# Attention and two feed-forward layers in one kernel: the values' products are issued one item later, transposed probabilities get a fourth room, and the masks read the thresholds where they are kept

## The chip, the core and the metric

The kernel runs on one core of one Trainium2 chip. The metric is device time in microseconds (us): the median of three runs of the kernel before is 1247.12 us (lowest 1243.89, highest 1250.25). One execution was profiled; it took 1249.53 us, of which the trace covers a span of 1247.8 us. Every time in this document that is read from the trace is on the clock of that span. PE is the matmul engine and PEld its weight load, DVE, ACT and POOL are the three engines that work on vectors, and SP issues the transfers (DMA). SPq in a row is SP's queue.

## The reference

Attention over 4 batches, 8 heads, 576 positions and head size 64, with a bias that a small network computes from the two positions; then two feed-forward layers over the 2304 tokens:

```python
scores = q @ k.T / sqrt(64)                              # (4, 8, 576, 576)
x = log1p(|i - j|) / log1p(max(i, 1))                    # (576, 576)
bias = relu(x[..., None] @ w1 + b1) @ w2                 # 32 hidden units, 8 heads
attn = softmax(scores + bias)                            # over j
y = (attn @ v) as (2304, 512)
y = (silu(y @ w_gate) * (y @ w_val)) @ w_out             # 512 -> 1536 -> 512
out = relu(y @ w_in) ** 2 @ w_out2                       # 512 -> 2048 -> 512
```

## The kernel before

**Numbers in two halves.** Almost every operand is held as two float16 numbers, a high part and the rest, and a product takes three matmuls (high by high, high by rest, rest by high). This is why one item of the attention needs a pair of probability halves, `pt`, and a transposed pair of them, `pT`.

**The attention's passes and items.** The 576 queries are worked on in five passes: t = 0, 1, 2 and 3 of 128 queries each, and a pass "m" in which the last 64 queries of two heads lie together. An item is one head of one batch (in pass m a pair of heads), so passes 0 to 3 have 32 items each and pass m has 16. This document numbers the 112 items from pass 1 on: 0 to 31 in pass 1, 32 to 63 in pass 2, 64 to 95 in pass 3 and 96 to 111 in pass m. Pass 0 is written differently: it takes its probabilities in float32, transposes them on PE and normalises by sums that it has beforehand.

**One item, step by step.** `scores` (L801): 4 matmuls (8 in pass m) into one of two PSUM rooms `qk`. `soft` (L820): DVE adds the bias and finds the extreme (L824), ACT takes the exponential into one of three rooms `s` (L832), then ACT or POOL, in turn, makes the high half in one of three rooms `pts` (L839, L836). `soft2` (L842): POOL makes the rest of it with two subtractions (L859 and L860, both recorded under the helper's line L220), then SP issues a transposing DMA from `pt` to `pT` (L861), one of three rooms. `weighted` (L864): 14 matmuls (28 in pass m) of `pT` with the values (L877). `normalise` (L882) divides on DVE, once per four items.

**The order in which an item's steps are written.** `attend` (L934) holds items back in two lists. In the turn of item k it writes the scores of k; then, if the list `pend_av` holds two items, the values' products of the oldest; then `soft` of k; then `soft2` of k-1, which puts k-1 on that list. So the products of item k-3 are written behind the scores of item k (L986). At the end of a pass the list is emptied: the products of all items that are left are written before the next pass begins (L1010).

**Between them.** `attend` is a generator, and `merge` (L1018) lets it take turns with `make_bias` for the next pass (the masks, L605, their products, L644, and the evacuation, L609), by costs written beside the `yield`s. The first feed-forward layer (`moe1`, L427: its matmuls are at L459 and L482) runs beside it as soon as 256 tokens (a "unit") are through the attention. The loop at L1321 picks which of the two streams is continued. The framework then takes this written order as priorities and sets the order of each engine's instructions itself, by its own model of their times; each engine then works its list strictly in order. A matmul that waits for its operand therefore holds up all matmuls behind it on PE, and a DMA issue that waits holds up all issues behind it on SP.

**Rooms.** Tiles of a pool that share a tag take turns in `bufs` rooms, and one that finds no free room waits for the last reader. The pool `att` lives through the attention. The pool `pre` (L1050) holds things of pass 0 and is closed at its end; the pool `strm` (L1128) is then opened in its place, for the keys, values and outputs of passes 1 to m. The second layer's weights (`weights2`, L1229) are loaded and decoded after the attention's pools are closed, and the second layer (`hidden`, `outputs`) runs from about 890 us to the end.

**The masks.** `bias_setup` computes one threshold per hidden unit and query into `thetas` (L546). `make_bias` (L586) sets one column of the spare tail of the pass's bias room to zero (L592), copies the pass's 128 thresholds there (L594) and compares a table with that copy, once per 32 keys of a query block (L605).

Of the kernel before, what the change touches and what calls it, by code (L numbers as in the profile page):

```python
# [11 lines left out]
F16 = mybir.dt.float16  # L12
# [9 lines left out]
B, H, S, D = 4, 8, 576, 64  # L22
DM, FF1, FF2 = 512, 1536, 2048
NT = B * S
P = 128
# [50 lines left out]
def tile_attention_moe(  # L76
# [4 lines left out]
    nc = tc.nc  # L81
# [20 lines left out]
    st = {}  # L102
# [291 lines left out]
    att = a_stack.enter_context(tc.tile_pool(name="att", bufs=2, side="right"))  # L394
# [108 lines left out]
        nc.sync.dma_start(y_d[m][P * t:P * t + P, :], yh.rearrange("p l e -> p (l e)"))  # L503


    BW = 8 * S + P
    rooms = [gv.tile([P, BW], F32, name="room0"), att.tile([P, BW], F32, name="room1", bufs=1)]
    w2a = rooms[0][:, 0:9 * 512].rearrange("p (a b) -> p a b", b=512)
    scrap = att.tile([P, 2112 + (TAB + TAB2) // 2], F32, name="scrap", bufs=1)
# [76 lines left out]
    def make_bias(t):  # L586

        merged = t == "m"
        i0, ni = (512, 64) if merged else (P * t, P)
        nh = 4 if merged else 8  # L590
        bias = rooms[{0: 1, 1: 0, 2: 1, 3: 0, "m": 1}[t]]
        nc.gpsimd.memset(bias[:, 8 * S:8 * S + 1], 0.0)  # L592
        theta = bias[:, 8 * S:8 * S + P // 2].bitcast(F16)[:, 0:ni]
        nc.vector.tensor_copy(theta, thetas[:, i0:i0 + ni])  # L594
        bias = bias[:, 0:nh * S].rearrange("p (h j) -> p h j", h=nh)
        st["bias", t] = bias
        xs = scrap[:, 1536:1536 + S]
# [242 lines left out]
        return s, pt  # L840

    def soft2(s, pt, warm=None):  # L842
        pT = att.tile([P, 10, P], F16, tag="pT", name="pT", bufs=3)
        if pt is None:
            pf = pT.rearrange("p a i -> p (a i)").bitcast(F32)
            tr = ps_qk.tile([P, 2, 512], F32, tag="qk", name="tr")
            if warm is not None and av_done[0] < 14:

                for _ in range(2):
                    nc.tensor.matmul(  # L850
                        tr[:, 0, :], ident_h, warm[:, 0:4, :], start=True, stop=True)
            for c in range(4):
                nc.tensor.transpose(tr[:, 0, P * c:P * c + P], s[:, P * c:P * c + P], ident)

            nc.tensor.transpose(tr[:, 1, 0:P], s[:, S - P:S], ident)
            nc.scalar.copy(pf, tr.rearrange("p a j -> p (a j)")[:, 0:640])
            return pf.rearrange("p (c i) -> p c i", i=P)

        rest_of(pt[:, 1, 64:S], s[:, 0:512], pt[:, 0, 0:512])  # L859
        rest_of(pt[:, 1, 0:64], s[:, 512:S], pt[:, 0, 512:S])  # L860
        nc.sync.dma_start_transpose(out=pT[:, 0:9, :], in_=pt.rearrange("p l j -> p (l j)"))  # L861
        return pT

    def weighted(t, pT, av, slot, vs):  # L864
# [69 lines left out]
    def attend(u0, t, bs, big, feed):  # L934
# [43 lines left out]
        for idx, (b, n) in enumerate(items):  # L978
# [4 lines left out]
            else:  # L983
                kts = [hold["k", b, n // 2][:, n % 2, :]]
            pq = scores(t, b, n, kts)
            if len(pend_av) == 2:  # L986
                yield from avstep(*pend_av.pop(0))
            yield 0.5
            total = None
# [499 lines left out]
```

## Time and profile before

| | |
|---|---|
| median of three runs | 1247.12 us |
| lowest, highest | 1243.89, 1250.25 us |
| the profiled execution, and its span | 1249.53 us, 1247.8 us |
| mean granted TensorE clock | 0.955 of full speed |
| PE busy | 1098.1 us, 88% of the span |
| PEld, DVE, ACT, POOL busy | 65%, 62%, 55%, 53% |
| the page's chain of waits, by engine | PE 44%, DMA 15%, POOL 9%, DVE 8%, ACT 5% |
| of it the transposes of the probabilities, and of the queries | 5%, 3% |

The shares are means over stages that differ: passes 1 to m run from 284 to 759 us, the second layer's weights are prepared around 770 to 890 us, and from 945 us on PE is busy nearly all the time. So each stage is read for itself. In a row that begins with an engine, a bracket at its end tells how long that engine sat idle before it and what ended the idle time.

### The profile page before, as it was taken

The numbers are of one execution on the slowest core, as the hardware profiler recorded it, in microseconds if no ns is written. First come the engines' busy times: TensorE is split into PE (matmuls) and PEld (weight loads), VectorE is DVE, ScalarE is ACT, GpSimd is POOL, SyncE is SP. The second block draws the span as 40 slices with busy tenths as digits, with TensorE's granted clock in tenths as the row PEclk, the third lists the DMA queues.
The fourth block names the chain that finished last, engine by engine and source line by source line (L and its number), as shares of the span: only waits on it lengthen the run. The fifth ranks groups of instructions, "written<-read, shape, count | busy, mean of one in ns | idle before, by whom it ended". The sixth has DMA issues, their size and how long they took to land.

```text
span 1247.8 us, 27388 instructions
## 1 busy us (share of the span) xinstructions
PE 1098.1 (88%) x10550; PEld 813.0 (65%) x10550; DVE 778.5 (62%) x1872; ACT 681.4 (55%) x1386; POOL 656.6 (53%) x842
## 2 busy tenths in 40 slices
PE   2587889999668889999997899979889999999998
PEld 2466778687457578686774767556348476584787
DVE  6998857787677566666575745886473442624423
ACT  4467877647667556656564543366452643616433
POOL 2532213269877688878685462136782541705423
PEclk9678889999989999999999999989999999999999
DMA  8867644219999999997979994660001010010100
GB/s 233 196 166 196 206 113 105 51 50 189 225 203 215 215 202 185 217 198 165 184 158 251 243 235 126 202 204 1 17 20 32 18 43 26 15 38 18 26 27 18
DMA packets 278079, 163.22 MB, mean 131 GB/s; under 512 B 233276, under 2 KB 246588, under 8 KB 277948
## 3 DMA queue, kind: packets, MB, share of 16 engines
q1 hardware_dynamic: 277948, 161.46, 56.1%
q8 instruction: 83, 1.36, 0.5%
q14 instruction: 48, 0.39, 0.1%
HBM read 92.13 MB, written 19.48 MB: 89 GB/s over the span
## 4 chain that ended last, share of the span: by engine, by line
PE 44%; DMA 15%; POOL 9%; DVE 8%; ACT 5%; issue 5%; SPq 1%; POOLq 0%; ACTq 0%; DVEq 0%
PE mm L1377 12%; PE mm L459 11%; PE mm L1409 10%; DMA pT<-pt 5%; DMA qT<-qs 3%; POOL pt L220 2%; PE mm L482 2%; POOL x L1189 2%; PE ma L1409 2%; PE av L877 2%; PE qk L815 1%; DMA w2s<-in_moe_w_out_dram 1%; DMA wr<-in_v_dram 1%; DMA w2s<-in_moe_w_in_dram 1%; DMA scrap<-in_moe_w_in_dram 1%
## 5 line engine op out<-in xcount | busy, mean ns | idle before, releaser
L459 PE MATMUL mm<-xT,wr 128*128 128x256 f16 x2400 | 292.5, 278 | 13.2 <-DVE th L470 6.8
L459 PEld LDWEIGHTS <-wr 128*128 128x128 f16 x2592 | 254.0, 100 | 54.7 <-issue 18.4
L1189 POOL TENSOR_TENSOR x<-x 128x256 f32<-128x256 f32 (+1 forms) x160 | 143.0, 905 | 177.9 <-ACT x L1386 171.5
L220 POOL TENSOR_TENSOR pt<-s,pt 128x512 f16<-128x512 f32 x224 | 172.8, 795 | 35.6 <-ACT pt L839 31.5
L220 POOL TENSOR_TENSOR z<-th,z 128x256 f16<-128x256 f32 x108 | 81.4, 755 | 122.9 <-ACT z L444 117.5
L482 PE MATMUL mm<-wr,z 128*128 128x512 f16 x612 | 142.1, 379 | 0.6 <-DVE th L470 0.6
L824 DVE CUSTOM_DVE_ANT_0 s<-qk,room 128x576 f32<-128x576 f32 x144 | 107.7, 749 | 38.7 <-PE qk L815 24.0
L1409 PEld LDWEIGHTS <-wr 128*128 128x128 f16 x1134 | 110.7, 98 | 20.5 <-DVE wr L1189 3.0
L832 ACT ACTIVATE s<-s,sc 128x576 f32<-128x576 f32 x112 | 85.9, 772 | 59.3 <-DVE sc L831 45.1
L1189 DVE TENSOR_TENSOR wr<-x,wr 128x768 f16<-128x768 f32 (+3 forms) x60 | 75.4, 1268 | 64.5 <-ACT wr L1196 63.4
L1377 PE MATMUL mm<-wr,w2r 128*128 128x512 f16 (+1 forms) x480 | 103.2, 366 | 6.5 <-ACT x L1382 6.5
L482 PEld LDWEIGHTS <-z 128*128 128x128 f16 x648 | 60.0, 98 | 65.4 <-issue 1.7
L1377 PE MATMUL mm<-wr,room 128*128 128x512 f16 (+1 forms) x480 | 100.1, 358 | 0.0
L877 PE MATMUL av<-vp,pT 128*128 128x65 f16 (+3 forms) x1792 | 69.3, 195 | 34.5 <-DMA pT<-pt 31.1
L605 DVE TENSOR_TENSOR scrap<-scrap,room 128x1024 f16<-128x1024 f16 (+1 forms) x108 | 85.3, 804 | 22.5 <-PE ma L644 16.5
L877 PEld LDWEIGHTS <-pT 128*128 128x128 f16 (+1 forms) x1792 | 60.1, 101 | 51.0 <-DMA pT<-pt 41.1
L621 POOL TENSOR_TENSOR scrap<-scrap 128x256 f32<-128x256 f32 (+1 forms) x90 | 64.4, 715 | 49.7 <-ACT scrap L620 45.6
L1377 PEld LDWEIGHTS <-w2r 128*128 128x128 f16 x480 | 47.7, 99 | 54.3 <-issue 10.4
L644 PEld LDWEIGHTS <-scrap 128*128 128x128 f16 x1440 | 60.3, 105 | 25.6 <-DVE scrap L605 13.9
L1377 PEld LDWEIGHTS <-room 128*128 128x128 f16 x480 | 47.1, 98 | 45.9 <-issue 0.7
L444 ACT CAST z<-th 128x256 f16<-128x256 f32 x108 | 42.9, 399 | 62.4 <-DVE th L470 62.0
L1428 ACT ACTIVATE ob<-ob,fac 128x256 f32<-128x256 f32 x36 | 17.8, 506 | 105.5 <-DVE ob L1427 105.5
(289 smaller groups left out, 2169.6 us busy)
## 6 DMA issues: line engine op xcount, KB each, us to landing
kp<-kT_d SPq DMA_DIRECT2D x64, 288.0 KB, 3.4
vp<-v_d SPq DMA_DIRECT2D x48, 325.0 KB, 3.5
w2s<-in_moe_w_out_dram SPq DMA_DIRECT2D x16, 512.0 KB, 3.9
wr<-in_moe_w_gate_dram SPq DMA_DIRECT2D x24, 256.0 KB, 4.5
wst<-in_moe_w_out_dram SPq DMA_DIRECT2D x12, 512.0 KB, 4.5
wr<-in_moe_w_val_dram SPq DMA_DIRECT2D x24, 256.0 KB, 4.1
v_d<-vp SPq DMA_DIRECT2D x16, 325.0 KB, 2.9
y_d<-yh SPq DMA_DIRECT2D x18, 256.0 KB, 2.6
```

Source lines behind the costliest of these rows:

```text
L220: nc.gpsimd.tensor_tensor(out=out_, in0=x, in1=hi, op=ALU.subtract)
L459: nc.tensor.matmul(pg[:, 256 * gi:256 * gi + 256], wr.parts(key, f // 4, cc, wl, P * (f % 4), P), mov(xl, cc), start=k == 0, stop=k == 11)
L482: nc.tensor.matmul(po, zall[:, f, zl, P * t:P * t + P], wr.parts("o", 0, f, wl), start=k == 0, stop=k == 3 * NF1 - 1)
L605: nc.vector.tensor_tensor(out=m[:, :, ni * e:ni * e + ni], in0=block(kb, i0, ni), in1=th, op=ALU.is_gt)
L621: nc.gpsimd.tensor_tensor(out=tmp[r], in0=tmp[r], in1=xb, op=ALU.mult)
L644: nc.tensor.matmul(pv[:, :, :, c:c + 4], m[:, a, :], bd[:, l], start=l == 0, stop=l == 1)
L824: nc.vector.tensor_tensor_reduce(out=s.rearrange("p (a j) -> p a j", a=2), in0=pq[:, :, 0:288], in1=bias[:, n].rearrange("p (a j) -> p a j ...
L832: nc.scalar.activation(s, s, AF.Exp, bias=nm, scale=-1.0)
L877: nc.tensor.matmul(av[r, slot, 0:cn], pT[:, 5 * l + c, r], vs[e][c][:, c0:c0 + cn], start=m == 0, stop=m == 13)
L1189: (nc.gpsimd if how else nc.vector).tensor_tensor(out=out_, in0=a, in1=b, op=op)
L1377: nc.tensor.matmul(ph[:, :n], w2r.parts("w", g // 4, cc, wl, P * (g % 4), P), yt[:, 4 * yl + cc, :], start=m == 0, stop=m == 11)
L1409: nc.tensor.matmul(po, HS[f][:, o:o + P], st["C7"][f][wl][:, b:b + 256], start=f == 0 and k == 0, stop=f == 7 and k == 2)
```

## The change

It has three parts. From pass 1 on, the list `pend_av` is let grow to three items before the oldest one's products are written, so that they stand behind the scores of the fourth item after theirs instead of the third. `pT` of these passes moves from the pool `att` (three rooms of ten 128-column blocks) to `strm`, with four rooms of nine blocks; pass 0 keeps three rooms, now in `pre`. And the masks compare with `thetas` itself: the copy, its zeroed column and the 128 spare columns of both bias rooms go.

```diff
-    BW = 8 * S + P
+    BW = 8 * S
...
-        nc.gpsimd.memset(bias[:, 8 * S:8 * S + 1], 0.0)
-        theta = bias[:, 8 * S:8 * S + P // 2].bitcast(F16)[:, 0:ni]
-        nc.vector.tensor_copy(theta, thetas[:, i0:i0 + ni])
+        theta = thetas[:, i0:i0 + ni]
...
     def soft2(s, pt, warm=None):
-        pT = att.tile([P, 10, P], F16, tag="pT", name="pT", bufs=3)
         if pt is None:
+            pT = pre.tile([P, 10, P], F16, tag="pT", name="pT", bufs=3)
...
-        nc.sync.dma_start_transpose(out=pT[:, 0:9, :], in_=pt.rearrange("p l j -> p (l j)"))
+        pT = st["strm"].tile([P, 9, P], F16, tag="pT", name="pT", bufs=4)
+        nc.sync.dma_start_transpose(out=pT, in_=pt.rearrange("p l j -> p (l j)"))
...
-            if len(pend_av) == 2:
+            if len(pend_av) == (2 if t == 0 else 3):
```

The number of matmuls is the same; DVE and POOL have five instructions less each. What moves is the order. In the changed program a line stands one or two lines higher (L815 is L813, L877 is L876, L605 is L603, L644 is L642).

On PE in pass 3, before: the products of item 73 (`pT_8957`), first-layer matmuls (`z`), the scores of item 77 (`qk_9097`), the products of item 74 (`pT_8993`).

```order
L877 LDWEIGHTS pT_8957
L877 MATMUL av_8972<-vp_8716,pT_8957 128x65
L877 MATMUL av_8972<-vp_8716,pT_8957 128x64
L482 LDWEIGHTS z_124
L482 MATMUL mm_9072<-wr_97,z_124 128x512
L815 LDWEIGHTS qT_8842
L815 MATMUL qk_9097<-kp_8997,qT_8842 128x288
L877 LDWEIGHTS pT_8993
L877 MATMUL av_8972<-vp_8875,pT_8993 128x65
L877 MATMUL av_8972<-vp_8875,pT_8993 128x64
```

The same place in the changed program; the scores of item 77 stand ahead of these rows, and `qk_9157` holds those of item 78. `pT_8928` is item 73, `pT_8976` item 74.

```order
L876 LDWEIGHTS pT_8928
L876 MATMUL av_9040<-vp_8722,pT_8928 128x65
L876 MATMUL av_9040<-vp_8722,pT_8928 128x64
L642 LDWEIGHTS scrap_116
L642 MATMUL ma_9100<-bd_118,scrap_116 128x16x4
L482 LDWEIGHTS z_124
L482 MATMUL mm_9028<-wr_97,z_124 128x512
L813 LDWEIGHTS qT_8818
L813 MATMUL qk_9157<-kp_9147,qT_8818 128x288
L876 LDWEIGHTS pT_8976
L876 MATMUL av_9040<-vp_8860,pT_8976 128x65
L876 MATMUL av_9040<-vp_8860,pT_8976 128x64
```

The products of item 74 moved behind the scores of item 78: 174 matmuls stand between its scores and its products, and 122 did before.

On PE where pass 1 ends and pass 2 begins, before: the products of item 26 (`pT_5349`), the first two scores of pass 2 (`qk_5751`, `qk_5823`), the products of item 27 (`pT_5437`).

```order
L877 LDWEIGHTS pT_5349
L877 MATMUL av_5297<-vp_5190,pT_5349 128x65
L877 MATMUL av_5297<-vp_5190,pT_5349 128x64
L815 LDWEIGHTS qT_5741
L815 MATMUL qk_5751<-kp_5743,qT_5741 128x288
L459 LDWEIGHTS wr_97
L459 MATMUL mm_5861<-xT_4615,wr_97 128x256
L815 MATMUL qk_5823<-kp_5743,qT_5741 128x288
L877 LDWEIGHTS pT_5437
L877 MATMUL av_5297<-vp_5190,pT_5437 128x65
L877 MATMUL av_5297<-vp_5190,pT_5437 128x64
```

The same two scores in the changed program (`qk_5745`, `qk_5815`); `pT_5606` is item 31, the last of pass 1.

```order
L876 LDWEIGHTS pT_5606
L876 MATMUL av_5608<-vp_5492,pT_5606 128x65
L876 MATMUL av_5608<-vp_5492,pT_5606 128x64
L482 LDWEIGHTS z_124
L482 MATMUL mm_6114<-wr_97,z_124 128x512
L813 LDWEIGHTS qT_5735
L813 MATMUL qk_5745<-kp_5737,qT_5735 128x288
L813 MATMUL qk_5815<-kp_5737,qT_5735 128x288
```

The first scores of pass 2 stood between the products of items 26 and 27 and now stand behind those of item 31: pass 1 is emptied first. From them to item 32's products there were 181 matmuls, and now there are 62.

On DVE at the start of the program, as a piece of the difference (`thetas` are the thresholds, `room_115` and `room_114` the two bias rooms).

```order
 L562 SCALAR_TENSOR_TENSOR sc<-sc,keep_197 128x16
 L566 COPY bd<-sc 32x16 x4
-L594 COPY room_115<-thetas 128x128
-L594 COPY room_114<-thetas 128x128
+L603 TENSOR_TENSOR scrap<-scrap,thetas 128x1024 x2
 L567 COPY bd<-sc 32x16 x4
-L605 TENSOR_TENSOR scrap<-scrap,room_115 128x1024 x3
```

The first two masks moved ahead of four small copies, and two copies are gone.

## Rows read from the trace of the kernel before

**Rows 1.** Windows: us; busy us of PE, PEld, DVE, ACT, POOL; clock; DMA; GB/s

```profile
284.00:334.00 50.00, 42.68 (x527) 30.05 (x525) 36.42 (x89) 33.30 (x75) 48.69 (x66) 1.00 1.00 206
334.00:380.00 46.00, 31.30 (x419) 25.62 (x419) 33.15 (x94) 28.72 (x65) 31.29 (x45) 0.85 1.01 214
380.00:472.00 92.00, 79.72 (x945) 61.41 (x943) 57.67 (x172) 55.33 (x115) 69.65 (x93) 0.98 1.02 210
472.00:664.00 192.00, 180.45 (x2172) 140.59 (x2171) 122.75 (x372) 118.27 (x263) 153.49 (x236) 0.99 0.95 188
664.00:710.00 46.00, 37.12 (x419) 26.94 (x415) 30.57 (x93) 21.63 (x41) 18.89 (x25) 0.96 1.06 254
```

**Rows 2.** The tile pT: count, ns min/median/max, first and last start; then waiters

```profile
L861 SPq DMA_TRANSPOSE pT<-pt x112: 1242/1363/3493, 284.2 to 754.0; - x112
L867 PE MATMUL av<-room,pT x120: 219/275/422, 124.7 to 217.8; 128*128 128x64 f32 x120
...
  PE av L877: 31.1, 32
...
DMA to landing us min/median/max: 3.2/4.0/7.5
```

**Rows 3.** Waits of PE, 284 to 334 us: total us, times, longest

```profile
PE av L877 <- DMA pT<-pt: 5.7, 7, 1.1
```

**Rows 4.** Waits of PE, 334 to 380 us

```profile
PE av L877 <- DMA pT<-pt: 7.6, 4, 3.9
```

**Rows 5.** Waits of PE, 380 to 472 us

```profile
PE av L877 <- DMA pT<-pt: 6.1, 9, 1.9
```

**Rows 6.** Waits of PE, 472 to 664 us

```profile
PE av L877 <- DMA pT<-pt: 5.3, 7, 1.4
```

**Rows 7.** Waits of PE, 664 to 710 us

```profile
PE av L877 <- DMA pT<-pt: 6.4, 5, 2.4
```

**Rows 8.** Waits of SP's queue, 284 to 760 us

```profile
SPq L861 <- POOL scrap L621: 27.8, 17, 2.9
...
SPq L770 <- PE av L877: 12.9, 12, 2.4
```

**Rows 9.** Timeline, start of the program: start us, us, instruction, count [idle before]

```profile
16.42 0.30 DVE L594 COPY room<-thetas 128x128 f16<-128x128 f16 x2
...
18.16 1.04 PE L644 MATMUL qk<-bd,scrap 128*128 128x64 f16 x16 [5.63 <-DVE scrap L605]
```

**Rows 10.** Timeline, pass 3: scores, transpose and products of item 75

```profile
575.14 0.63 PE L644 MATMUL ma<-bd,scrap 128*128 128x64 f16 x16
...
578.20 0.65 PE L815 MATMUL qk<-kp,qT 128*128 128x288 f16 x4
...
587.96 1.32 SPq L861 DMA_TRANSPOSE pT<-pt  x1
...
592.16 0.60 PE L877 MATMUL av<-vp,pT 128*128 128x65 f16 x14 [1.42 <-DMA pT<-pt]
```

**Rows 11.** Timeline, pass 1 to 2: scores and products of item 32

```profile
399.18 0.65 PE L815 MATMUL qk<-kp,qT 128*128 128x288 f16 x4 [0.15 <-DMA kp<-kT_d]
...
401.12 2.78 PE L459 MATMUL mm<-xT,wr 128*128 128x256 f16 x24
...
413.49 4.91 PE L482 MATMUL mm<-wr,z 128*128 128x512 f16 x22
...
418.24 0.31 PE L877 MATMUL av<-vp,pT 128*128 128x65 f16 x5
```

**Rows 12.** Timeline, pass 3 to m: scores and products of item 96

```profile
667.22 0.68 PE L810 MATMUL qk<-kp,qT 128*64 128x288 f16 x8
...
686.37 0.63 PE L877 MATMUL av<-vp,pT 128*64 128x65 f16 x28 [1.66 <-DMA pT<-pt]
```

**Rows 13.** The chain that ended last: start us, us, what

```profile
773.14 4.43 DMA w2s<-in_moe_w_in_dram
...
1046.82 41.44 PE mm L1377 x192
```

## The prediction

> **What bounds the kernel now.** I read the windows by stage first, since the shares of the whole span mix unlike stages. The change touches passes 1 to m. There PE is the busiest engine, but not evenly [rows 1]: it is busy for 180.45 of 192 us in the long middle stretch (472 to 664 us), 79.72 of 92 before that, and only 31.30 of 46 between 334 and 380 us, where its clock also fell to 0.85. At the head of pass 1 another engine is full: POOL with 48.69 of 50 us.
>
> Next I asked what PE waits for. The list of the tile `pT` puts 31.1 us of idle PE in front of the values' products, with the transposed probabilities as the releaser [rows 2]. A transpose lands 4.0 us after its issue at the median, 7.5 at worst. Split by stretch the 31.1 us are 5.7, 7.6, 6.1, 5.3 and 6.4 [rows 3 to 7], and none after 710 us. This is all that later products can take out; PE has the same matmuls before and after.
>
> Then the items. In the middle stretch, item 75's scores end at 578.85 us and its products start at 592.16, of which PE idled 1.42 [rows 10]: the item's own way (softmax, rest, transpose) took 13.3 us and the matmuls between filled 11.9 of them. So the length of two ways is what matters: L, from an item's scores to the landing of its `pT`, which other engines set, and W, the PE work that the order puts between scores and products. PE idles where L is longer than W.
>
> Last, the chain of waits: behind the attention come loads of the second layer's weights, then PE without a gap [rows 13]. What PE gains or loses before 760 us therefore reaches the end nearly one for one.
>
> **The change part by part.** *The masks.* Five copies and five settings of a column go. Only the first two copies stand on a path: they cost DVE 0.30 us just before the first masks, for which PE was idle 5.63 us [rows 9]. Term: -0.3 us, bounds -0.3 and 0. The masks themselves keep shape, type and count, and both operands stay in the same memory; I price that at nothing.
>
> *The move of `pT`.* Same transposes, same size; pass 0 keeps three rooms. The new rooms lie where pass 0's things lay, so the first could have to wait for pass 0's products; those had ended soon after 217.8 us and the first transpose is issued at 284.2 [rows 2]. Zero, with 66 us to spare.
>
> *The fourth room.* SP's waits say whether the third room was short. Those of the transposes (L861) end with POOL's work, while waits for PE's products stand only at the loads of the values, L770 [rows 8]. No transpose waited for a room by this list; the room alone is worth nothing, and it only permits the new order. Those value loads move with the products: the room that they wait for comes free one item later, and what needs them is issued one item later too. Queued behind them on SP are transposes, so a load that waits longer would hold these up; the 12.9 us of such waits were spread over 12 loads, and I put the difference at zero.
>
> Here I weighed a rule of the Trainium skill, Perfetto Trace Analysis, section Optimization Strategy: a gap that repeats on the engine that should be full can mean that there is not enough memory for the next tile, such as too few buffers. By it most of the 31.1 us would go, and the sum would be about -31 in place of mine. The trace disagrees: the repeated gap ends with a landing, and not with a room.
>
> *The order on PE.* This is the change. I counted the matmuls that the built order puts between each item's last score and its first product, and priced them by rows: 0.11 us for a first-layer matmul of 256 columns and 0.22 of 512, 0.13 for a score (4 in 0.65 us, with the last one's tail), 0.04 for a product or a mask product [rows 10, 11]. W then comes out, before and after, as:
>
> - items 0 to 13 (to 334 us): 16.0 and 16.0. The order is the same instruction for instruction: here the framework's own times put the products, not the list's length. The 5.7 us stay.
> - items 14 to 23 (334 to 380): 11.3 and 11.7. Three waits make up the 7.6 us, the longest 3.9. Term -1, bounds -3 and +1.5 (one item, 19, has 1.5 us less in front of it).
> - items 24 to 45 (380 to 472): 14.5 falls to about 12.8. Pass 1 is now emptied before pass 2 begins. Item 32 shows the most: 19.0 us from the start of its scores to its products [rows 11], filled with 17.7 us of work, of which 11.9 are left. But this L was long because, by the order, the products of five older items were still outstanding when its scores were issued; with three, item 75 needed 13.3, and now item 32 has none ahead of it. If L shrinks as W does, nothing is lost; if not, each of about six rounds of this stretch (92 us by some 15) loses 1.7, that is 10 us. I take +2, near the first end, because the row with fewer items ahead has the shorter L.
> - items 46 to 61 and 66 to 91 (most of 472 to 664): 12.6 and 13.8 rise to 16.6 and 17.4. Item 75's 1.42 us of waiting vanish under 3.5 us more of work, and so do the others: the longest wait is 1.4 and the added work is three to four. Of the 5.3 us I leave 0.7 to items 62 to 65, where pass 2 is emptied, and take most of the rest. Term -4, bounds -4.6 and -2.
> - items 62 to 65: 13.3 falls to 11.2. Term +0.7, bounds 0 and +2.
> - items 92 to 98 (664 to 710): 11.4 and 12.4, but item 96 has 2 us less in front of it, and it waited 1.66 us with an L of 18.5 [rows 12]. Term -0.5, bounds -3 and +3.
> - items 99 to 111: 14.5 and 17.4; no wait to remove.
>
> Sum: -0.3 - 1 + 2 - 4 + 0.7 - 0.5 = -3.1 us. Against the profiled execution that is 1249.5 - 3.1 = 1246.4. That execution was 2.4 us above the median of the runs, 1247.1; from the median the sum gives 1244.0, which is my forecast. Less than 0.5%, 6.2 us, can't be told from no change by runs that spread from 1243.9 to 1250.3.
>
> Why so little of 31 us? The order gets its slack where PE hardly waits (5.3 us in 192), and gets next to none where it waits most (334 to 380, 664 to 710), since there the framework placed the products when it thought them ready, whatever the list.
>
> **The rivals.** *Faster, 1235.* The slack also reaches the stretches where PE waits most: a PE that is later in one round gives the front of the next rounds time, and the waits of 334 to 472 and 664 to 710 halve. That is half of 7.6 + 6.1 + 6.4, 10 us, with 4 in the middle: 14 less two lost at the emptied passes makes -12. The clock of 0.85 between 334 and 380 us speaks for some more, if the wait of 3.9 us is what lowered it. Against it stands the order, which puts only 0.4 us of new work there, and POOL, full just before. The least that this kind could give is all waits kept and -4; the most is all 25.4 us behind 334, or 1222.
>
> *A room was short, 1216.* If transposes started late for want of a room, the fourth ends every wait for them: all 31.1 us, 1247.1 - 31.1 = 1216. Against it stands that no wait of L861 ends with PE [rows 8], and that the order of items 0 to 13 is unchanged, so that their 5.7 us can only go by an earlier issue. This is what the page's rule would make of the gaps.
>
> *Slower, 1256.* The mechanism is the emptied passes. Items 24 to 45 lose 1.7 us of cover in each of six rounds because their L doesn't shrink, +10; items 62 to 65 and 96 lose 2 each, as the order takes from them; the middle gives 4 back, and the rest -1. That makes +9 on 1247.1, 1256. For it: SP's transposes wait for POOL, 27.8 us with one of its mask steps as the releaser alone [rows 8], and POOL is busy for 69.65 of 92 us there [rows 1], which the number of items ahead doesn't change. Against it: PE has first-layer matmuls to put there, and the row of item 75 has the shorter L. It decides from about 10 us of loss at the emptied passes on; below that the middle's gain keeps it within 0.5%.
>
> *The change does not do what it says, 1247.* The products follow the fourth item's scores only where the framework let the written order decide. If its own times decide everywhere that matters, nothing happens but -0.3. For it: items 0 to 13 are untouched. It lies within 0.5% as the forecast does.
>
> **How the numbers follow.** I give the forecast 0.42 and the change that does nothing 0.15, the faster rival 0.20, the short room 0.03, the slower 0.20. The first two stay within 0.5% but for some 0.03 of the first that reach below -6.2 us. So faster by over 0.5% 0.26, within 0.5% 0.54, slower 0.20. The forecast's own range is 1239 to 1249. For eight times in ten I reach to the values of the faster and the slower rival: 1234 to 1256, which also holds the terms' bounds but for the case that nearly all of them fall on one side.
>
> **What would show it.** In the profile after: PE's idle time in front of the products between 472 and 664 us falls from 5.3 to under 2 us, and item 75 or its neighbours wait for nothing; before 334 us it stays near 5.7. The stretch from item 24 to item 45 takes 92 us and two more, not ten more. SP's waits at L770 do not grow by more than a few us. The end of the attention moves from 759 to about 756 us and all behind it by the same. I am wrong if the middle stretch keeps its waits in spite of 4 us more of work, if the waits of 334 to 380 us go without new work in front of them, or if the time changes behind 760 us or before 284 us by more than 2 us.

## The result and the profile after

The changed kernel takes 1254.9 us (median of 15 runs, 1249.4 to 1263.0) against 1249.2 for the kernel before: ratio 1.0058, 95% interval [1.0033, 1.0082]. The medians differ by 5.8 us and the ratio makes it about 7 us slower, where I had forecast 3 us less. Timed a second time (e5 below) the ratio was 1.0050 [1.0031, 1.0070].

The head of the page of the changed kernel, the profiled execution's span and the busy time of each engine:

```profile
span 1253.9 us, 27368 instructions
PE 1097.1 (87%) x10550; PEld 811.9 (65%) x10550; DVE 778.5 (62%) x1867; ACT 682.9 (54%) x1386; POOL 651.3 (52%) x837
```

The windows of the changed kernel, in the stretches of [rows 1], with the start in front and the whole attention (first scores of pass 1 to the last products) behind:

```profile
0.00:284.00 284.00, 220.61 (x2243) 180.97 (x2244) 227.13 (x560) 180.33 (x378) 99.03 (x120) 0.95 0.56 148
284.00:334.00 50.00, 42.13 (x526) 29.69 (x522) 35.95 (x90) 32.06 (x73) 46.01 (x64) 0.97 1.04 211
334.00:380.00 46.00, 34.78 (x416) 28.19 (x417) 34.66 (x100) 31.24 (x70) 33.71 (x47) 0.81 0.95 217
380.00:472.00 92.00, 77.82 (x936) 59.17 (x934) 57.23 (x166) 53.56 (x112) 65.33 (x89) 0.98 0.98 199
472.00:664.00 192.00, 177.19 (x2109) 138.92 (x2107) 117.56 (x360) 116.95 (x259) 150.66 (x233) 0.97 0.90 180
664.00:710.00 46.00, 38.56 (x442) 27.37 (x440) 32.00 (x102) 22.12 (x43) 20.98 (x30) 0.96 1.06 252
...
271.00:764.00 493.00, 432.24 (x5265) 328.27 (x5262) 314.84 (x924) 289.61 (x619) 355.40 (x511) 0.96 0.94 199
```

PE is busy for 177.19 of 192 us in the long middle stretch, where it had 180.45 [rows 1] and was to gain 4. Between 380 and 472 us it lost 1.9. The same matmuls ran, so what is missing there runs later.

The waits of PE in the changed kernel (total us, times, longest), which answer to [rows 3 to 7] and the end of pass m; the lines between "..." are the stretches 284 to 334, 334 to 380, 380 to 472, 472 to 664, 664 to 710 and 700 to 765 us:

```profile
PE av L876 <- DMA pT<-pt: 3.9, 7, 1.2
...
PE av L876 <- DMA pT<-pt: 4.4, 4, 2.8
...
PE av L876 <- DMA pT<-pt: 11.2, 13, 1.8
...
PE av L876 <- DMA pT<-pt: 6.8, 4, 4.5
PE mm L459 <- DVE yh L501: 5.3, 2, 4.6
PE ma L642 <- ACT room L624: 2.4, 3, 1.0
...
PE av L876 <- DMA pT<-pt: 3.3, 3, 1.4
PE av L876 <- issue: 1.9, 1, 1.9
...
PE qk L808 <- DVE room L265: 3.7, 1, 3.7
```

In sum 28.5 us of waiting for transposed probabilities are left of 31.1 [rows 2]; in a second profile of the changed kernel (e5) it is 32.8. Three things are to be seen. Between 380 and 472 us the waits for transposed probabilities nearly doubled (6.1 to 11.2). In the middle they did not go but came together: one of 4.5 us in place of the longest of 1.4. And waits of 4.6 and 3.7 us stand where no products are, in front of the first layer and of scores. (The last row names DVE, as the one that came last; a load of keys landed at the same time, as is shown below.)

The timeline shows where these waits come from and what follows them. PE, SP's queue, ACT and DVE of the changed kernel (start us, us, instruction, count, in brackets the idle time before): item 62's products, then what leads to the wait of 4.6 us, then to that of 3.7:

```profile
531.10 1.01 PE L876 MATMUL av<-vp,pT 128*128 128x65 f16 x28
536.65 0.94 PE L876 MATMUL av<-vp,pT 128*128 128x65 f16 x14 [4.55 <-DMA pT<-pt]
537.41 4.67 PE L459 MATMUL mm<-xT,wr 128*128 128x256 f16 x21
...
595.64 5.59 SPq L860 DMA_TRANSPOSE pT<-pt  x2
601.33 1.31 SPq L757 DMA_TRANSPOSE qT<-qs  x1
...
606.11 0.63 ACT L744 ACTIVATE qs<-qf 128x512 f16<-128x512 f32 x1 [5.22 <-DMA qT<-qs]
...
606.77 0.43 DVE L745 SCALAR_TENSOR_TENSOR qs<-qf,qs 128x256 f16<-128x256 f32 x1 [5.12 <-ACT qs L744]
607.23 0.23 DVE L752 COPY qs<-qs 128x256 f16<-128x256 f16 x1
607.48 0.75 DVE L501 SCALAR_TENSOR_TENSOR yh<-mm,sc,yh 128x512 f16<-128x512 f32 x1
...
608.28 1.01 PE L459 MATMUL mm<-xT,wr 128*128 128x256 f16 x4 [4.62 <-DVE yh L501]
...
714.34 0.65 SPq L765 DMA_DIRECT2D kp<-kT_d  x1
715.33 3.77 SPq L757 DMA_TRANSPOSE qT<-qs  x1
719.15 1.25 SPq L765 DMA_DIRECT2D kp<-kT_d  x1
...
723.10 0.79 PE L808 MATMUL qk<-kp,qT 128*64 128x288 f16 x8 [3.69 <-DVE room L265]
```

Behind the wait of 4.55 us 21 first-layer matmuls take 4.67 us; in [rows 11] 24 of them took 2.78. PE ran them at the lower of its two clock levels (the granted clock between 538 and 542 us is 0.50), so the wait cost about 4.67 - 21 x 2.78 / 24 = 2.2 us more than its own length. The second group is a chain through four engines: two transposes of probabilities hold SP's queue for 5.59 us, a transpose of queries is behind them, ACT's next cast of queries waits for its room, DVE stands behind ACT, and the DVE instruction that would empty PE's result stands behind that. The third is of another kind. Of the two loads of keys the one that released PE was issued at 714.34, ahead of the transpose of queries; the row of this load alone:

```profile
L765 SPq DMA_DIRECT2D kp<-kT_d x1: 647/647/647, 714.3 to 714.3; - x1
...
  PEld L808: 3.8, 1
...
DMA to landing us min/median/max: 8.7/8.7/8.7
```

It landed 8.7 us after its issue, at 723.05, and PE went on at 723.10. Two loads of the second layer's weights of 512 KB each had been issued at 710.87 and 711.40, and the DMA is full from 714 to 718 us (its share in that window is 1.21). In e5 it is the same (8.6 us, behind two such loads); in the kernel before and in e1 the last of these loads was issued at 702.5 and 699.9. That the weights' loads held up the keys is likely by this, but no run tested it.

The granted clock (last column but two) around item 62 in windows of 10 us, changed kernel:

```profile
520.00:530.00 10.00, 9.31 (x105) 8.19 (x104) 6.25 (x24) 6.04 (x12) 6.53 (x10) 1.00 0.90 217
530.00:540.00 10.00, 5.45 (x66) 4.39 (x65) 2.52 (x7) 2.94 (x6) 3.82 (x6) 0.79 0.87 178
540.00:550.00 10.00, 10.00 (x95) 8.43 (x94) 5.39 (x24) 4.49 (x10) 3.44 (x6) 0.87 0.62 138
```

### The profile page after: what moved, and what is told of

Read it like the earlier page. It is cut to its first block, busy times and chain, and to the rows that moved or that the text cites. A ratio compares the mean times of both kernels' runs of the same rounds, so it can differ in the third digit from the quotient of the medians.

```text
span 1253.9 us, 27368 instructions
## 1 busy us (share of the span) xinstructions
PE 1097.1 (87%) x10550; PEld 811.9 (65%) x10550; DVE 778.5 (62%) x1867; ACT 682.9 (54%) x1386; POOL 651.3 (52%) x837
## 4 chain that ended last, share of the span: by engine, by line
PE 42%; DMA 19%; DVE 15%; POOL 11%; issue 6%; ACT 5%; SPq 2%; POOLq 0%; DVEq 0%; ACTq 0%
PE mm L1376 12%; PE mm L1408 10%; PE mm L459 8%; PE mm L482 3%; DMA pT<-pt 3%; POOL pt L220 3%; DMA wr<-in_moe_w_gate_dram 2%; DMA qT<-qs 2%; POOL x L1188 2%; DMA wr<-in_v_dram 2%; PE ma L1408 2%; DMA scrap<-in_moe_w_in_dram 2%; PE av L876 1%; DVE s L822 1%; PE qk L813 1%
## 5 line engine op out<-in xcount | busy, mean ns | idle before, releaser
L876 PE MATMUL av<-vp,pT 128*128 128x65 f16 (+3 forms) x1792 | 71.0, 196 | 31.6 <-DMA pT<-pt 28.5
L603 DVE TENSOR_TENSOR scrap<-scrap,thetas 128x1024 f16<-128x1024 f16 (+1 forms) x108 | 85.1, 803 | 15.8 <-PE ma L642 9.3
L876 PEld LDWEIGHTS <-pT 128*128 128x128 f16 (+1 forms) x1792 | 62.2, 103 | 45.2 <-DMA pT<-pt 37.0
L642 PEld LDWEIGHTS <-scrap 128*128 128x128 f16 x1440 | 60.1, 105 | 25.3 <-DVE scrap L603 11.2
```

Of the source, the lines that this page charges most:

```text
L603: nc.vector.tensor_tensor(out=m[:, :, ni * e:ni * e + ni], in0=block(kb, i0, ni), in1=th, op=ALU.is_gt)
L642: nc.tensor.matmul(pv[:, :, :, c:c + 4], m[:, a, :], bd[:, l], start=l == 0, stop=l == 1)
L876: nc.tensor.matmul(av[r, slot, 0:cn], pT[:, 5 * l + c, r], vs[e][c][:, c0:c0 + cn], start=m == 0, stop=m == 13)
```

## The experiments

Every kernel was timed in rounds beside the kernel before; times are medians, ratios those to the kernel before. The theories had letters as I went, and they are kept in the quoted expectations. Theory A was the prediction's slower rival: a pass that is emptied leaves too little work in front of the products.

**Which part of the change loses (e1 to e5).** e1 is the changed kernel with two waiting items, so it has the new rooms and the masks' edit, but not the order. e2 is the kernel before with the masks' edit alone.

```diff
# e1
-            if len(pend_av) == (2 if t == 0 else 3):
+            if len(pend_av) == 2:
# e2 (on the kernel before)
-    BW = 8 * S + P
+    BW = 8 * S
...
-        nc.gpsimd.memset(bias[:, 8 * S:8 * S + 1], 0.0)
-        theta = bias[:, 8 * S:8 * S + P // 2].bitcast(F16)[:, 0:ni]
-        nc.vector.tensor_copy(theta, thetas[:, i0:i0 + ni])
+        theta = thetas[:, i0:i0 + ni]
```

> The changed kernel with its new rooms and its masks that read the thresholds, but with two waiting items again in all passes, so that values' products follow the second next item's scores. Theory A (the order lost about 10 us at the pass changes and behind them, and the masks' edit gained the 4 us by which PE's progress leads at 275 us): the order's loss goes, the lead stays: about 1245 us, ratio to before 0.997. Theory B (the lead at 275 us is chance of one execution, and the order alone lost the 6 to 7 us): 1249 us, ratio 1.000. Theory C (the loss comes from the rooms or from where they lie now, not from the order): it stays at about 1256, ratio 1.006.

Measured: 1246.0, ratio 0.9984 [0.9966, 1.0001].

> The kernel before with one edit: masks read the thresholds directly, without the copy and the extra columns of the two bias rooms. Theory A: the start is 4 us shorter and all behind it by as much: 1245 us, ratio 0.997, with item 0's scores near 271 us instead of 275. Theory B: 1249 us, ratio 1.000, item 0's scores within 1.5 us of before. Theory C says nothing of this edit; with e1 at 1.006 and this one at 1.000 the rooms are to blame.

Measured: 1245.7, ratio 0.9969 [0.9954, 0.9985]. Theory C falls: the rooms cost nothing that the intervals could tell. The masks' edit gains 2 to 6 us, more than the 0.3 of my sum. Where it gains can't be read from one trace: item 0's scores ended at 272.6 us in e2, but anywhere between 271 and 278 in the changed kernel and in e1 and e3 to e9, whose engines run the same instructions in the same order up to there. The order's share is 1.0058 / 0.9984 = 1.0074, or 9 us lost.

This also settles the rival that a room was short. e1 has four rooms and two waiting items, and between its first scores and last products PE still waits 28.0 us for transposed probabilities. So the Trainium skill's reading of repeated gaps (Perfetto Trace Analysis, Optimization Strategy: too few buffers may be behind them) does not hold here.

```diff
# e3
-            if len(pend_av) == (2 if t == 0 else 3):
+            if len(pend_av) == (3 if t == 1 else 2):
# e4
+            if len(pend_av) == (2 if t in (0, 1) else 3):
```

> The changed kernel with three waiting items in pass 1 alone (items 0 to 31), two in all others. Theory A (each emptied pass loses): only the change from pass 1 to pass 2 loses, by the progress of PE some 4 us between 400 and 475 us: 1245 + 4 = 1249, ratio 1.000. Rival D (the loss is not at the emptied passes but in the later passes' interior, where units of the first layer become ready one item later): pass 1 costs nothing, as e1: ratio 0.997.

Measured: 1248.9, ratio 1.0014 [0.9999, 1.0030].

> The changed kernel with three waiting items in passes 2, 3 and m alone (items 32 to 111), two in pass 1. Theory A: the change from pass 2 to pass 3 loses its 6 us, with PE's wait of over 3 us at item 62's products, and the stretch behind another 3 or 4: 1245 + 10 = 1255, ratio 1.005. Rival D: the same total, but without the wait at item 62.

Measured: 1246.0, ratio 0.9991 [0.9972, 1.0011]; PE still waits 4.0 us at item 62. Pass 1 loses 3 to 4 us over e1, as A says; the later passes lose nothing by themselves, which no theory said. Together that is less than the 9 us. So the wait at item 62 by itself can't be most of the loss.

> The changed kernel once more, beside the same runs of the kernel before as the next three. e3 and e4 cost 3.7 and 0.9 us over e1, together 4.6, while the changed kernel stood 9 above e1 when it was first timed. If the two parts simply add up, it is at 1250.5 here, ratio 1.002; if the passes 1 and 2 lose together what neither loses alone (pass 2 begins empty behind a pass that was emptied of four), it is again at 1255, ratio 1.006.

Measured: 1254.4, ratio 1.0050. So it is no chance of the first timing; pass 1 and the later passes lose more together. e5's trace has the same waits: 10.0 us for transposed probabilities between 380 and 472 us, 3.8 at item 62, 2.8 for the first layer at 606, 2.9 for keys at 721.

**Is it the emptying of passes? (e6 to e9)** e6 keeps two waiting items at the end of each pass. e7 and e8 hand what waits to the next pass, with three and with two waiting items; e9 has three in passes 2 and 3 alone.

```diff
# e6
+            while len(pend_av) >= (2 if t == 0 or idx > len(items) - 4 else 3):
...
# e7; e8 has 2 for 3; e9 has (3 if t in (2, 3) else 2), with while
...
-        pend_soft = None
-        pend_av = []
+        pend_soft, pend_av = (None, []) if t == 0 else kept.pop()
...
             if len(pend_av) == (2 if t == 0 else 3):
-                yield from avstep(*pend_av.pop(0))
+                f, *p = pend_av.pop(0)
+                yield from f(*p)
...
+        if t not in (0, "m"):
+            kept.append((pend_soft, pend_av))
+            return
...
```

> The changed kernel, but the last three items of each pass again keep only two waiting, so that three items and not four are emptied at its end. By the order PE has 13.4 us of work in front of the products of items 62 to 65 as in the kernel before (changed: 11.2), while items 24 to 45 keep 12.8 as in the changed kernel. Theory A (idle time comes where the order leaves less work than an item's way takes): the wait of 4.5 us at item 62 goes, with the lower clock behind it, and the wait of items 24 to 45 stays: 5 us less than the changed kernel, 1250, ratio 1.001. Rival D (the passes' interior or the later ready units lose the time): 1255, ratio 1.006.

Measured: 1256.6, ratio 1.0088 [1.0060, 1.0115]. The wait at item 62 went (none over 0.82 us there, and no lower clock), as the count of the order said. The time did not follow.

> The changed kernel with three waiting items, but passes 1, 2 and 3 are not emptied: what waits is handed to the next pass and its products follow that pass's first scores; only pass m is emptied. By the order the work in front of the products is 13.9 us for items 24 to 45 (changed: 12.8), 15.6 for items 62 to 65 (11.2), 15.8 for items 92 to 98 (12.4), and 16.6 and 17.1 between, as in the changed kernel. Theory A: the losses at both emptied passes go and the middle's gain stays: below e1, at 1240 us, ratio 0.993, with PE's waits for transposed probabilities between items 24 and 98 at half of before. Rival E (the way of an item grows with what is put in front of its products, since softmax has one rate, so that cover can't help): 1250 or more, ratio 1.002.

Measured: 1252.5, ratio 1.0049 [1.0029, 1.0068].

> As e7 (passes 1 to 3 not emptied), but with two waiting items as in the kernel before. Work in front of the products: 13.3 us for items 24 to 45 and 12.0 for items 62 to 65, 13.8 for 92 to 98, 13.2 between. Theory A: emptying three items cost the kernel with two little (1.7 us of waiting at items 62 to 65, part of 6 at 92 to 98): 1 to 3 us below e1, 1244, ratio 0.997. If e7 and e8 are alike and both well below e1, the emptying alone is what matters, and the third waiting item gives nothing.

Measured: 1244.3, ratio 0.9977 [0.9955, 0.9999]. This pair shows most. PE's waits between 472 and 664 us, e7 and then e8 (`yh` is the first layer's output on its way out of PE's result room, L905 the scale of a finished unit, L470 the first layer's middle):

```profile
PE mm L459 <- DVE yh L501: 6.5, 2, 3.5
PE ma L131 <- DVE sc L905: 4.5, 3, 1.9
PE mm L459 <- DVE th L470: 2.4, 3, 1.6
```

```profile
PE av L876 <- DMA pT<-pt: 7.4, 6, 1.8
PE av L876 <- issue: 1.2, 2, 1.0
PE mm L459 <- DVE yh L501: 1.1, 1, 1.1
```

With three waiting items and no emptied pass, every wait for transposed probabilities is gone there, which is what I had forecast of the change. But e7 is 8 us slower than e8. Theory A falls as the cause of the whole. Rival E had the time (1250 or more), but not the mechanism: the cover did work.

The whole attention of e8, e7, e1 and e5 (windows; the second number is the length, the third PE's busy time, the third from the end the clock):

```profile
276.00:748.00 472.00, 420.23 (x5217) 320.49 (x5214) 317.75 (x922) 287.93 (x616) 356.07 (x511) 0.98 0.98 208
```

```profile
274.00:764.00 490.00, 433.05 (x5216) 328.68 (x5214) 320.42 (x921) 288.12 (x616) 357.79 (x510) 0.95 0.95 200
```

```profile
274.00:756.00 482.00, 427.49 (x5250) 324.71 (x5250) 316.86 (x922) 286.45 (x616) 356.58 (x511) 0.97 0.96 204
```

```profile
272.00:762.00 490.00, 429.80 (x5270) 327.47 (x5267) 318.05 (x924) 289.31 (x619) 356.86 (x512) 0.97 0.94 200
```

In these profiled executions e7 is 18 us longer than e8 here, 5.2 of it idle (57.0 to 51.8) and 12.8 busy, for the same matmuls. That is more than the 8 us of the medians: the profiled execution of e7 (1258.05 us) was the second slowest of its 12, that of e8 (1240.24) the fastest of its 12. The clock goes with the busy part, 0.95 to 0.98. In this stretch e7 has 13 waits of PE of 1.5 us and more (31.0 us in all) and e8 has 7 (15.4 us). Behind some of them the clock fell. From e7, PE's wait and the windows behind it:

```profile
553.34 0.27 PE L131 MATMUL ma<-ident,sc 128*1 128x128 f32 x1 [1.93 <-DVE sc L905]
...
554.00:558.00 4.00, 4.00 (x31) 3.06 (x29) 2.35 (x13) 2.68 (x5) 1.72 (x3) 0.57 0.92 221
558.00:562.00 4.00, 4.00 (x62) 3.48 (x60) 3.28 (x10) 2.17 (x5) 3.02 (x5) 1.00 0.47 83
```

The clock is 0.57 in the four us behind this single wait and full again in the next four. But a wait of the same length in e8 was followed by a full clock:

```profile
448.16 1.14 PE L813 MATMUL qk<-kp,qT 128*128 128x288 f16 x8 [1.93 <-DMA kp<-kT_d]
...
446.00:450.00 4.00, 1.89 (x30) 1.29 (x26) 2.36 (x9) 2.88 (x7) 3.41 (x5) 1.00 1.13 188
450.00:454.00 4.00, 3.84 (x49) 3.39 (x47) 3.93 (x12) 3.29 (x7) 3.66 (x7) 1.00 0.92 228
```

In e1 it stayed at 1.00 behind a wait of 3.15 us too (at 601.10, windows 598 to 602 and 602 to 606). So the length of a wait alone does not tell whether the clock falls.

The changed kernel against e1 was profiled twice, both times near its median. Idle time is 493 - 432.24 = 60.8 us, and 60.2 in e5, to 482 - 427.49 = 54.5 in e1: 6 us more each time. Busy time is 5 us more, and 2 in e5, whose mean clock is that of e1. So the idle time is the part that came twice. PE's idle time between the first scores and the last products, by what PE ran next (us, summed from the timelines):

| | products, for `pT` | scores | first layer | small matmuls for scales (L131, L169) | masks' products | rest | sum |
|---|---|---|---|---|---|---|---|
| before | 31.1 | 7.2 | 10.7 | 3.8 | 0.6 | 3.8 | 57.2 |
| e1 | 28.0 | 8.1 | 10.5 | 3.4 | 1.4 | 3.1 | 54.5 |
| changed | 28.5 | 10.8 | 9.4 | 3.4 | 4.3 | 4.4 | 60.8 |
| changed again (e5) | 32.8 | 9.9 | 8.2 | 3.4 | 3.7 | 2.2 | 60.2 |
| e8 | 28.2 | 11.6 | 5.2 | 2.8 | 0.7 | 3.3 | 51.8 |
| e7 | 18.9 | 11.9 | 12.7 | 8.9 | 1.9 | 2.7 | 57.0 |

In the changed kernel the waits for `pT` did not fall at all against e1 (its two profiles differ by 4.3 us here), and scores and masks wait more. In e7 they did fall, by 9, and the first layer with its scales waits 13.6 more.

> As e8 (passes 1 to 3 not emptied), but three waiting items in passes 2 and 3 (items 32 to 95) and two in passes 1 and m. Work in front of the products by the order: items 46 to 61 17.2 us (e8: 13.2), 62 to 65 15.6 (12.0), 66 to 91 17.1 (13.1); items 24 to 45 13.9 (13.3). Rival F (it is pass 1 or pass m with three that loses; in the interior of passes 2 and 3 the third item takes the waits away, 7.5 us of them in e8, and costs nothing): 1239, ratio 0.993. Rival G (the third item costs wherever it is, because PE's other work then stops in longer pieces, 2 us and more, on the first layer's results, and the clock falls behind each of them): the waits for transposed probabilities go and waits in front of the first layer take their place, 1249, ratio 1.001.

Measured: 1251.3, ratio 1.0028 [1.0006, 1.0050]: the value of rival G, the third item costs 6 us over e8. It does not cost that wherever it is, though: with emptied passes three items from pass 2 on (e4) cost 1 us over e1, which the intervals can't tell from nothing.

**Does the first layer's place decide? (e10, e11, e13 to e18)** A table (LEAD) says how far the attention's stream is ahead of the first layer's. These runs add a constant to it; e17 adds it to e7, and e18 takes 0.7 off in e8.

```diff
-        lead = base is not None and pos["a"] >= base + float(np.interp(pos["m"], *LEAD))
+        lead = base is not None and pos["a"] >= base + 1.4 + float(np.interp(pos["m"], *LEAD))
```

> The changed kernel with the first layer's stream held back by 1.4 units of the attention's stream, which is one item. Rival D (the units of the first layer become ready one item later with three waiting, and the table that places the first layer's work was written for two): the old distance is back, the loss goes: 1247, ratio 1.000. Rival G: no such relation; the holes move, 1252 to 1256, ratio 1.005.

> e1 (two waiting items) with the first layer's stream held back by the same 1.4 units. It is the control for e10: by rival D two waiting items with this shift are one item off the other way and lose: 1250 or more, ratio 1.003. If the time only depends on chance in the order, e10 and e11 move by some us in any direction; if neither moves by more than 2 us, the table's distance is not what matters.

> The changed kernel (three waiting items) with the first layer's stream 1.4 units earlier against the attention's. Rival D (the table's distance must grow with the waiting items): further off, 1258 or more, ratio 1.008. Chance of the order, with no rule: anywhere from 1247 to 1258.

> The changed kernel with the first layer's stream 2.8 units later. Rival D: the best distance for three waiting items lies one item behind that for two; 2.8 is one too many, so between e10 and the unshifted changed kernel or worse: 1252 to 1256. If instead 1248 or less comes out, distance is what the third item lacked, and more than one item of it.

> e1 (two waiting items) with the first layer's stream 1.4 units earlier. With e1 (1246) and e11 (1.4 later, 1252): if this too is 1249 or more, the table's distance is at its best for two waiting items and any move off it costs 3 to 6 us; that is what a change of the number of waiting items would run into. If it is 1246 or less, e11's loss is not a matter of a best distance.

> e1 with the first layer's stream 2.8 units later: by the same rule more than e11, 1254 or more, ratio 1.006; by chance of the order anywhere from 1245 to 1257.

Measured, as ratios to the kernel before (half-widths of the intervals 0.002 to 0.003):

| Shift of the first layer | -1.4 | 0 | 1.4 | 2.8 |
|---|---|---|---|---|
| two waiting items | 0.9981 (e15) | 0.9984 (e1) | 1.0042 (e11) | 1.0068 (e16) |
| three waiting items | 1.0139 (e13) | 1.0050 (e5) | 1.0031 (e10) | 1.0047 (e14) |
| three over two | 1.0158 | 1.0066 | 0.9989 | 0.9979 |

The third item's cost hangs on this distance: 20 us, 8 us, and then nothing. It falls to nothing because two waiting items lose there (6 us and more with a later first layer); three gain little, and 1.0050, 1.0031 and 1.0047 are not told apart. With three an earlier first layer loses 11. e11, e13 and e16 came out as rival D said, e10 (1250.8) lies between the values of D and G, and e15 (1245.9) is what its expectation had named against a best distance: two waiting items are as fast 1.4 earlier as at the table's distance. At none of the four distances are three waiting items as fast as two at theirs. That other orders of the same work lose several us by chance is not excluded: two items with a shift alone (e11, e16) lose as much as the change did.

> e7 (three waiting items, passes 1 to 3 not emptied) with the first layer's stream 1.4 units later, as in e10. Work in front of the products by the order: 13.7 us for items 24 to 45, 16.3, 17.2, 16.9, 17.4 and 19.4 behind them. If the distance and the emptying are two separate parts of the loss, they add: 2.5 us won over e7, 1249.5, ratio 1.002, and the rest, some 4 us over two waiting items, stays. If the third item costs nothing once both are mended, it reaches e8's 1244, ratio 0.998. If the distance was chance, 1252 or more.

Measured: 1259.3, ratio 1.0102 [1.0075, 1.0130]. The expectation was a miss: the shift that put e10 0.0019, or 2.4 us, below e5 (not clear of the intervals) loses 6 to 7 in e7's kernel. So "one item later" is no rule to mend it by, and the two parts do not add.

> e8 (two waiting items, passes 1 to 3 not emptied) with the first layer's stream 0.7 units earlier, between e1 and e15: the version that all runs so far point to. If the best distance for two lies between -1.4 and 0: 1242 to 1244, ratio 0.996; if the curve is flat there: as e8, 0.998.

Measured: 1242.2, ratio 0.9960 [0.9941, 0.9980], the fastest of all: two waiting items, masks that read the thresholds, no emptied passes, the first layer 0.7 earlier. It beats the kernel before by 5 us and the changed one by 11 to 12. It is not told apart from e8 by more than the intervals.

**SP's queue (e12).**

```diff
     def prep_q(b, t, a):
+        with tc.high_priority():
+            prep_q_(b, t, a)
+
+    def prep_q_(b, t, a):
...
```

> The changed kernel with the preparation of queries (their load, cast and transpose) at high priority in the order. In the changed kernel SyncE's queue held a transpose of queries behind transposes of probabilities that waited for POOL (5.6 us at 595.6), ACT and DVE stood behind it, and PE waited 4.6 us for the first layer's results at 603.4; at 719.2 it waited 3.7 us for keys whose load stood behind a transpose of queries. Rival H (the one queue of SyncE makes the long waits): both waits go, with the lower clock behind them: 8 us less, 1247, ratio 1.000. Rival G in its plain form (holes come back in another place): 1252 or more, ratio 1.004.

Measured: 1265.3, ratio 1.0148. A miss that tells little: the priority also moved the first queries ahead of the masks, item 0's scores ended at 282.6 us in place of 271 to 278, and between them and the last products PE waited 15.2 us for keys and queries (e5: 7.3). Whether the one queue makes the long waits was not settled. The expectation also had the keys of the wait at 719 wrong: their load stood ahead of the transpose of queries and landed late, as shown above.

## Why the prediction was wrong, term by term

The mechanism of the sum was idle time: put 4 us of other work in front of the products, and their waits go and come back nowhere. The term for items 46 to 61 and 66 to 91 is where that failed, and the terms for the emptied passes had the wrong size.

- *Masks, -0.3 (bounds -0.3 and 0).* Mis-sized. e2 gives -2 to -6 us. I priced only the copies; the edit also changes the order of the start on PE and DVE, which I had not counted. That the gain comes from there is not shown.
- *Rooms and the move, 0.* Right: e1 against e2 differs by 0.0015, inside both intervals. Room alone takes few of the waits away (28.0 us left in e1 of 31.1). My reading that no transpose's wait ended with PE was a little off: the full list behind [rows 8] has two such waits, 1.3 and 1.0 us.
- *Items 0 to 13, 0, and 14 to 23, -1 (-3 to +1.5).* The waits fell by 1.8 and 3.2 us (5.7 [rows 3] to 3.9, 7.6 [rows 4] to 4.4), and in e5 by 1.3 and 1.2. e1, with two waiting items, has 4.8 and 6.7, so most of this is not the order's.
- *Items 24 to 45, +2 (0 to +10).* The waits rose by 5.1 us (6.1 [rows 5] to 11.2; 10.0 in e5). I took the near end, because L was to shrink with W. It did: from an item's last score to its landing it takes 14.2 us on average in place of 16.0 (over the items whose landing the trace tells), while W fell by 1.7 by my count. But the mean is not what waits: 13 items come too late instead of 9, and the mean time from landing to products fell from 1.0 to 0.7 us.
- *Items 46 to 61 and 66 to 91, -4.* This is the step that failed first. The mechanism was right: `pT` now lies ready for 3.4 and 4.9 us on average before its products (before 1.0 and 2.2). But L grew too, to 13.3 and 13.0 us on average (11.1 and 11.9 before), and there was less to win than I put in: 1.7 of the 5.3 us [rows 6] belonged to items 62 to 65, and of the other 3.6 us 2.3 are still there. And I took it, without a reason, that the work put in front of the products is missed nowhere else. It is: 2.4 us of waiting for a mask's room came new (2.1 in e5), and the waits for the first layer, 5.2 us in six pieces before, are 5.3 in two, the longest 4.6 (2.8 in e5, 2.7 before). e7 shows the step bare: all the waits for `pT` are gone between 472 and 664 us, and the kernel is 8 us slower than e8.
- *Items 62 to 65, +0.7 (0 to +2).* The largest miss, outside its bounds: item 62 waits 4.55 us, 2.9 more than these four items did together, and the lower clock behind it costs 2.2 more (3.8 us of waiting in e5).
- *Items 92 to 98, -0.5.* The waits fell by 3.1 (6.4 [rows 7] to 3.3; 4.8 in e5), at the bound; beside them stands a wait of 1.9 us for which the profile names no releaser.
- *Items 99 to 111, 0.* Wrong: 3.7 us of waiting for keys (2.9 in e5), by a load that took 8.7 us to land. The sum had no term for what else the DMA moves: two loads of the second layer's weights now stand just ahead of these keys. What I "put at zero", the waits of the values' loads for PE, fell from 12.9 us [rows 8] to 6.0.
- *The clock.* No term had it. I read the clock of 0.85 between 334 and 380 us as a detail of one stretch. In the changed kernel PE was busy 5 us longer than in e1, at a mean clock of 0.96 against 0.97; in e5 it was 2 us longer, at 0.97.

I had said that I would be wrong if the middle stretch kept its waits in spite of 4 us more of work; it did (5.3 to 6.8). Behind the attention nothing changed, as I had said: from the last products to the end it is 488 us before and 490 after. The start was 4 us ahead, which says nothing where executions of one order spread over 7. The slower rival came true in its time (1256) and partly in its mechanism: it named items 24 to 45 and 62 to 65, which did lose. But e6 and e7 show that mending the emptied passes does not give the time back with three waiting items.

What is shown: the order loses 8 to 9 us, the masks gain 2 to 6; the loss lies between the first scores and the last products, some 6 us of it as idle time in both profiles, and PE busy 2 to 5 us longer with the same matmuls; the third item's cost depends on where the first layer's work stands. What stays open: why the waits move from the products to the first layer, the scores and the masks when three items wait, and whether there is more to it than one order against another. One long wait was followed to SP's queue and one to a late landing (above), but no run took either away cleanly.

## What to carry to other kernels

The sum of an engine's waits at one kind of instruction is what a change could win at most; moving work in front of them takes it from other places, so ask at each what covers the gap that it leaves. A long wait can cost more than its length (4.55 + 2.2 us at item 62), but a count of long waits did not rank these kernels: e18, the fastest, has 11 of 1.5 us and more (25 us) in its attention, and e6, 14 us slower, has 9 (22 us). Where a profiled execution is the fastest or slowest of its kernel, compare its parts with a second one before a cause is read from it. A queue depth and the pacing of a second stream are one setting, not two: change them together, and compare each depth at its own best pacing.

## What the hardware showed that I had not expected

PE's granted clock fell behind single waits of 1.9 to 4.6 us in stretches that were otherwise nearly full (1.93 us before the 0.57 in e7; 0.79 in the window of the 4.55 us in the changed kernel), but not behind all of them: 1.93 us in e8 and 3.15 us in e1 were followed by 1.00. e8 went through 7.4 us of waits in six pieces, none over 1.8, between 472 and 664 us, and kept the full clock. Programs that start alike took from 271 to 278 us to item 0's scores, which is as much as the whole effect under study: only the timed rounds could tell the parts apart.
